# Order and bank use of the first down stage of a pooled-attention and gated-MLP kernel

## The chip, the cores and the metric

The kernel runs on one core of a Trainium2 chip. The metric is the device time in microseconds (us) of one execution; lower is better. The engines have their own instruction queues: TensorE (PE, with its weight loads listed apart as PEld), VectorE (DVE), ScalarE (ACT), GpSimd (POOL) and SyncE (SP, which only issues transfers here). Matmul results go to PSUM, which this kernel splits into three pairs of banks (`banks[0]` to `banks[2]`) and two single banks (`obanks`).

## The reference

Keys and values are averaged over 8 neighbouring positions, attention runs over the 72 pooled positions, and its output goes through two matrix products with g = h cos(h) between them.

```python
# batch 8, heads 8, sequence 576, head_dim 64; d_model 512, d_ff 2048
k_p = k.reshape(B, H, Sp, pool, D).mean(axis=3)      # pool 8, Sp 72
v_p = v.reshape(B, H, Sp, pool, D).mean(axis=3)
scores = scale * np.matmul(q, k_p.transpose(0, 1, 3, 2))
attn = softmax(scores)
attn_out = np.matmul(attn, v_p)
x = attn_out.transpose(0, 2, 1, 3).reshape(B * S, H * D)   # 4608 x 512
h = x @ w_in
g = h * np.cos(h)
return g @ w_out
```

## The kernel before

The 4608 tokens are worked in nine tiles of 512 (`NT`, `TILE`). Each pass t of the main loop (L563) has an up stage and a down stage. The up stage multiplies the tile's columns of `xT` by `w_in` (L354), eight pairs of 512-wide results, each into a bank pair given by `up_bank`; ScalarE takes the cosine (L364) and VectorE multiplies (L368) into `g_sb`. The down stage multiplies `g_sb` by `w_out`. From t = 1 on it is done by seven half-sized products (L432) that need sums of weight blocks, w1 to w4, made by `put_weights` (L388); at t = 0 it is done directly (`down_mm`, L371), 64 matmuls numbered n: 4 row blocks `ms` times 16 chunks `fc`, the chunks lying in four blocks `w_out_sb[0..3]`. Each row block is summed in one PSUM bank, copied out by VectorE (`down_out`, L376) and stored through SP.

Attention is woven into these stages. Batch 0 is worked before the loop (L534 to L560). At t = 0 the down stage also works batch 1: a list `fill` of pairs (n, what) puts pieces ahead of matmul n. `S_(i, bank)` is the scores of part `us[i]` of batch 1: four matmuls (L234) into a bank pair and an exp on ScalarE (L241). `V_(i, bank)` is its values: four matmuls (L269), two Ln (L275) and one exp (L276) on ScalarE for the inverse of the sums, and then a multiply on VectorE in two halves (L280), which reads the bank pair and writes columns of `xT`. With a third argument, the multiply is put into the list `later` and issued by a later entry of `fill`. REST is the remaining 64 rows of batch 0, and `pool_v_mm` pools the values of batch 1.

The schedule is manual: each engine runs its instructions in the order of the code, and waits come from the data and the buffers. So the place of a `put_weights` or of a multiply in the code is its place in VectorE's queue. A bank pair that `values` has used is free once its multiply has read it.

The up stage of t = 1 starts with `up_mm` into `banks[0]`, then `banks[2]`, `banks[1]` and the two `obanks`. Its columns of `xT` are the 64 rows of REST and most of batch 1, so it needs the four multiplies of `us` as well.

At the end of t = 0 GpSimd issues the loads of batch 2 and then pools its keys and values by additions (`pool_first`, L157; `pool_rest`, L163 to L169). The blocks of w_out are loaded by GpSimd's queue in the order 0, 2, 1, 3 (L517 and L522).

The first keys of batch 0 are pooled on TensorE (`pool_k_mm`, L178) and copied into `kk` by `put_kk` (L151) in four casts, all on one engine.

Of the kernel before, what the change touches and what calls it, by code (L numbers as in the profile page):

```python
# [9 lines left out]
FP32 = mybir.dt.float32  # L10
# [10 lines left out]
def kernel(  # L21
# [9 lines left out]
    nc = tc.nc  # L31
    B, H, S, D = q.shape
    Sp = S // POOL
    d_model = H * D
# [112 lines left out]
    def put_kk(b, ps, pj0, pj1, copy):  # L147
        for a in range(2):
            for r in range(2):
                j = key_slot(b, 2 * pj0 + a, r)  # L150
                copy(out=kk[b % 2][half[r], j:j + pj1 - pj0, 0:Sp], in_=ps[half[a]])  # L151

    def pool_first(b, which):

# [16 lines left out]
    def pool_k_mm(b, bank, pj0, pj1):  # L171

        kb = staged["k", b]
        ps = bank[:, 0:(pj1 - pj0) * Sp].rearrange("p (j n) -> p j n", n=Sp)
        for pj in range(pj0, pj1):
            for t in range(ROW):
                for rows in half:
                    nc.tensor.matmul(ps[rows, pj - pj0, :], lhsT=kb[rows, pj, t, :], rhs=groups[rows, t, :],  # L178
                                     start=(t == 0), stop=(t == ROW - 1))
        return lambda copy: put_kk(b, ps, pj0, pj1, copy)  # L180
# [42 lines left out]
    def scores(b, u, pair):  # L223
        scores_mm(b, u, pair)
        scores_exp(b, u, pair)
# [145 lines left out]
        nc.tensor.matmul(o, lhsT=g_sb[:, fc, ms * 128:(ms + 1) * 128],  # L371
                         rhs=w_out_sb[fc // 4][:, fc % 4, :], start=(fc == 0), stop=(fc == FFCH - 1))

    def down_out(t, ms, ps):
        o = msb.tile([128, 2, d_model], FP32, name="o_two", tag="o_two", bufs=2)[:, 0]
        nc.vector.tensor_copy(out=o, in_=ps)  # L376
        rows_of = out.rearrange("(b p t) m -> b t p m", b=B, t=ROW)
        for i, rows in enumerate(half):
            b_, pos = divmod((t * TILE + ms * 128) // 64 + i, ROW)
            nc.sync.dma_start(out=rows_of[b_, ORDER[pos]], in_=o[rows])  # L380
# [151 lines left out]
    early_inverses += ["p1_sb", "v_sb", "q_sb"] * 3  # L532

    warm_up(10, obanks[0])  # L534
    pool_k_mm(0, obanks[1], 0, 2)(vec)
    warm_up(2, banks[1][:, 0, :])
    puts = q_transpose_mm(0, banks[2][:, 0, :], 0, 5), q_transpose_mm(0, obanks[0], 5, 9)
    puts[0](vec)
# [24 lines left out]
    for t in range(NT):  # L563
        b = t + 1
        if t > 0:

            for fp in up_order(t)[0:2]:
                up_mm(t, fp, 0, 2)
        for n, fp in enumerate(up_order(t)):
            up_mm(t, fp, 2 if n < 2 else 0)  # L570
            between = ()
            if t == 0:
                if fp == 4:
                    puts = pool_k_mm(1, obanks[0], 0, 2), pool_k_mm(1, obanks[1], 2, 4)
                elif fp in (5, 6):
                    g0 = 9 * (fp - 5)
                    puts = q_transpose_mm(1, obanks[0], g0, g0 + 5), q_transpose_mm(1, obanks[1], g0 + 5, g0 + 9)
                if fp in (4, 5, 6):
                    puts[0](vec)
                    between = ((puts[1], act),)  # L580
            up_g(t, fp, between)

            late = {5: (1,), 6: (3,)} if t == 1 else {4: (1, 2), 5: (3,)}
            sums = {} if t == 0 else late if b < B else {3: (1, 2), 4: (3,), 5: (4,)}
            put_gs(*[(i, 0) for i in sums.get(n, ())])
            if 0 < t and b < B:
                if n == 0:
                    q_transpose(b)
                    k_transpose(b)
                elif n == 2:  # L590
                    pool_rest(b, "v")
                    if b + 1 < B:
                        nc.gpsimd.tensor_copy(out=gate, in_=kk[b % 2][0:1, H - 1, 0:1])
                        load_q(b + 1)
                        load_kv(b + 1, "v", v)
            if n == 2:
                while stores:
                    stores.pop(0)()
        mms = [(ms, fc) for ms in range(4) for fc in range(FFCH)]
        if t == 0:  # L600
            mms = [(ms, fc) for hm in range(2) for cg in (0, 2, 1, 3) for ms in range(2 * hm, 2 * hm + 2)
                   for fc in range(4 * cg, 4 * cg + 4)]


        def S_(n, bank):
            return lambda: scores(b, us[n], banks[bank])

        later = []

        def V_(n, bank, wait=None):  # L610
            return lambda: values(b, us[n], banks[bank], wait)

        fill = []
        if t < B:
            exp_tables()
            fill = [(1, lambda: scores(t, REST, banks[2])), (16, lambda: values(t, REST, banks[1]))]
        if t == 0:
            fill = [(2, lambda: scores(t, REST, banks[1])), (2, S_(0, 0)), (8, lambda: pool_v_mm(1, banks[2])),
                    (8, lambda: values(t, REST, banks[1])),
                    (8, lambda: put_weights(0, nc.vector, (3, 2))), (8, S_(1, 0)), (8, V_(0, 2)),  # L620
                    (18, S_(2, 1)), (18, lambda: put_weights(0, nc.vector, (4,))),
                    (18, lambda: put_weights(1, nc.vector, (1,))), (21, V_(1, 0, later)), (26, S_(3, 2)), (32, lambda: later.pop()()),
                    (32, V_(2, 1)), (40, V_(3, 0))]
        if t == FIRST:
            early_inverses.clear()
        if t < FIRST:
            fi = 0
            for n, (ms, fc) in enumerate(mms):
                while fi < len(fill) and fill[fi][0] <= n:
                    fill[fi][1]()  # L630
                    fi += 1
                down_mm(obanks[ms % 2], ms, fc)
                if fc == FFCH - 1:
                    down_out(t, ms, obanks[ms % 2])
                if n == 4:
                    put_weights(0, nc.vector, (1,))
                elif n == 36:
                    put_weights(1, nc.vector, (3,))
            put_weights(1, nc.vector, (2, 4))
        else:  # L640
            products, reads = down_products(t)

            def product(i, j=0, k=2 * HF):
                for mm in products[i][j:k]:
                    mm()

            later = []

            u0, u1, u2, u3 = [(b, CHUNKS[i], banks[j]) for i, j in enumerate((2, 1, 0, 1))]
            ur = (t, REST, banks[2])  # L650

            def scores_of(*parts):
                for part in parts:
                    scores_mm(*part)
                for part in parts:
                    scores_exp(*part)

            def muls():
                while later:
                    later.pop(0)()  # L660

            steady, rest = b < B, t < B
            if rest:
                exp_tables()

            product(0, 0, 12)
            product(1, 0, 4)
            product(0, 12)
            reads[0]()
            if steady:  # L670
                scores_of(u0, u1, u2)
            elif rest:
                scores_of(ur)
            product(1, 4)
            if t == 1:
                put_g(2, 0)
            put_gs((1, 1), (2, 1))
            if not steady:
                reads[1]()
            put_gs((3, 1), (4, 1))  # L680
            if steady:
                reads[1]()
                put_g(4, 0)
                values_rows(*u0)
            product(2)
            reads[2]()
            if steady:
                values_rows(*u1)
                values_rows(*u2)
            product(3)  # L690
            reads[3]()
            muls()
            product(4)
            reads[4]()
            muls()
            if steady:
                scores_of(ur, u3)

            product(5, 0, 6)
            if rest:  # L700
                values(*ur, later)
            product(5, 6, 12)
            muls()
            if steady:
                values_rows(*u3)
            product(5, 12)
            reads[5]()
            muls()
            product(6)
            reads[6]()  # L710
        if t < B:
            sin_tables()
        if b + 1 < B:
            if t == 0:
                load_kv(b + 1, "k", k)
                load_q(b + 1)
                load_kv(b + 1, "v", v)
            else:

                nc.gpsimd.tensor_copy(out=gate, in_=g4[0:1, 0, 0:1])  # L720
            pool_first(b + 1, "k")
            if t != 1 and b + 2 < B:
                load_kv(b + 2, "k", k)
            pool_rest(b + 1, "k")
            if t == 1:
                load_kv(b + 2, "k", k)
            pool_first(b + 1, "v")
# [28 lines left out]
```

The softmax here doesn't subtract the row's maximum and nothing guards it: scores larger than these inputs give would overflow.

## Time and profile before

| what | value |
|---|---|
| time, median of 3 runs | 285.4 us (284.73 to 286.28) |
| time of the profiled execution | 284.58 us |
| its span, first to last instruction | 282.8 us |
| granted TensorE clock, mean | 0.999 |
| first down matmul of t = 0 | 33.45 us |
| first up matmul of t = 1 | 53.05 us |
| one down matmul, start to start | 0.216 us |

Times in views count from the start of the span. A timeline row gives the start, the time it covers, the engine, the line, the operation, the written and read tiles, shapes, and the number of instructions merged into it; brackets give the idle time before it and what ended that. In the chain of waits each row is what the end of the program depended on at that time.

### The profile page before, as it was taken

How to read it: one execution, taken by the hardware profiler on the slowest of the kernel's cores; microseconds unless marked ns; L12 is line 12 of the kernel's file. 1: busy time of each engine (PE TensorE's matmuls, PEld its weight loads, DVE VectorE, ACT ScalarE, POOL GpSimd, SP SyncE). 2: the span in 40 equal slices, each digit the busy share in tenths (PEclk: the TensorE clock that was granted, in tenths of full speed). 3: DMA queues.
4: the chain of work that ended last, by engine and by line, in shares of the span. 5: the costliest groups of instructions: out<-in, count | busy, mean ns of one | idle time of the engine just before them, and what ended most of it. 6: DMA issues, size and time to landing. Idle time of an engine off the chain costs nothing.

```text
span 282.8 us, 5887 instructions
## 1 busy us (share of the span) xinstructions
PE 275.2 (97%) x2378; PEld 185.4 (66%) x2378; DVE 212.6 (75%) x313; ACT 167.3 (59%) x199; POOL 132.1 (47%) x146
## 2 busy tenths in 40 slices
PE   7899999999999999999999999999999999999994
PEld 3555554456875687568756975688558855875683
DVE  5448769889946995699568966896689669846972
ACT  3787798368357735774567556655666555436600
POOL 8542114995599259934993389539910000000000
PEclk9999999999999999999999999999999999999999
DMA  7999999795739798997688959882660260005015
GB/s 153 201 206 209 212 207 216 132 190 84 118 60 163 125 215 140 136 175 155 101 148 146 189 80 163 156 174 52 125 148 3 58 148 19 2 21 127 2 37 112
DMA packets 56202, 36.13 MB, mean 128 GB/s; under 512 B 35440, under 2 KB 51312, under 8 KB 56176
## 3 DMA queue, kind: packets, MB, share of 16 engines
q0 software_dynamic: 18208, 18.07, 40.8%
q1 hardware_dynamic: 37328, 17.18, 29.7%
q10 hardware_dynamic: 640, 0.52, 0.8%
q8 instruction: 18, 0.29, 0.4%
q14 instruction: 8, 0.07, 0.1%
HBM read 36.70 MB, written 9.44 MB: 163 GB/s over the span
## 4 chain that ended last, share of the span: by engine, by line
PE 92%; ACT 3%; DMA 2%; DVE 1%; issue 1%; POOL 0%; POOLq 0%; DVEq 0%
PE bank L354 39%; PE obank L432 33%; PE obank L354 5%; PE obank L371 4%; PE bank L234 3%; DMA q_b<-in_q_dram 2%; PE bank L296 2%; PE bank L432 2%; ACT ex L241 1%; PE bank L269 1%; PE obank L178 0%; DVE g_sb L368 0%; PE obank L215 0%; PE bank L186 0%; ACT cos L364 0%
## 5 line engine op out<-in xcount | busy, mean ns | idle before, releaser
L354 PE MATMUL bank<-xT,w_in_sb 128*128 128x512 bf16 x512 | 113.8, 379 | 0.1
L364 ACT ACTIVATE cos<-bank,half_pi 128x1024 f32<-128x1024 f32 x64 | 70.4, 1115 | 55.9 <-PE bank L354 55.9
L354 PEld LDWEIGHTS <-w_in_sb 128*128 128x128 bf16 x576 | 64.9, 113 | 57.4 <-issue 0.3
L368 DVE TENSOR_TENSOR g_sb<-bank,cos 128x1024 bf16<-128x1024 f32 x64 | 77.0, 1221 | 30.5 <-ACT cos L364 30.3
L157 POOL TENSOR_TENSOR half_sums<-kv_st 72x512 f32<-72x512 bf16 x48 | 54.4, 1158 | 8.4 <-DMA kv_st<-in_k_dram 8.0
L241 ACT ACTIVATE ex<-bank 72x1024 bf16<-72x1024 f32 (+1 forms) x40 | 35.0, 931 | 30.0 <-PE bank L234 30.0
L432 PEld LDWEIGHTS <-g 128*128 128x128 bf16 x512 | 47.8, 98 | 5.8
L432 PE MATMUL obank<-w,g 128*128 128x256 bf16 x368 | 42.6, 272 | 0.0
L432 PEld LDWEIGHTS <-g_sb 128*128 128x128 bf16 x384 | 37.0, 98 | 6.4
L163 POOL TENSOR_TENSOR half_sums<-half_sums 72x512 f32<-72x512 f32 x24 | 30.0, 1273 | 0.0
L432 PE MATMUL obank<-w_out_sb,g_sb 128*128 128x256 bf16 x240 | 28.9, 273 | 0.0
L398 DVE TENSOR_TENSOR g<-g_sb 128x1024 bf16<-128x1024 bf16 x32 | 21.9, 685 | 0.3
L720 POOL COPY gate<-g 1x1 bf16<-1x1 bf16 x5 | 0.9, 180 | 37.9 <-DVE inv_rows L299 37.9
L280 DVE TENSOR_TENSOR xT<-bank,inv 64x256 bf16<-64x256 f32 x14 | 5.9, 422 | 15.4 <-ACT inv L276 15.4
L301 DVE TENSOR_TENSOR x_rows<-bank,inv_rows 128x512 bf16<-128x512 f32 x24 | 16.6, 692 | 0.8
L432 PE MATMUL obank<-w_out_sb,g 128*128 128x256 bf16 x112 | 15.6, 273 | 0.0
L432 PE MATMUL obank<-w,g_sb 128*128 128x256 bf16 x128 | 15.3, 272 | 0.0
L371 PE MATMUL obank<-w_out_sb,g_sb 128*128 128x512 bf16 x64 | 15.2, 379 | 0.0
L354 PE MATMUL obank<-xT,w_in_sb 128*128 128x512 bf16 x64 | 15.1, 379 | 0.0
L234 PE MATMUL bank<-qT,kk 64*72 64x128 bf16 (+2 forms) x288 | 12.3, 221 | 0.1
L332 ACT ACT_TABLE_LOAD x9 | 11.5, 1283 | 0.9 <-PEq L740 0.7
L234 PEld LDWEIGHTS <-kk 64*72 64x72 bf16 x288 | 8.7, 110 | 5.1 <-issue 3.4
(99 smaller groups left out, 270.0 us busy)
## 6 DMA issues: line engine op xcount, KB each, us to landing
out_dram<-o_two SPq DMA_DIRECT2D x64, 128.0 KB, 2.4
kv_st<-in_v_dram POOLq DMA_DIRECT2D x8, 576.0 KB, 12.3
kv_st<-in_k_dram POOLq DMA_DIRECT2D x7, 576.0 KB, 8.1
q_b<-in_q_dram POOLq DMA_DIRECT2D x6, 576.0 KB, 7.6
w_in_sb<-in_moe_w_in_dram POOLq DMA_DIRECT2D x4, 512.0 KB, 13.5
w_out_sb<-in_moe_w_out_dram POOLq DMA_DIRECT2D x4, 512.0 KB, 18.6
q_b<-in_q_dram POOLq DMA_DIRECT2D x4, 288.0 KB, 12.3
g_sb<-in_k_dram SPq DMA_DIRECT2D x1, 576.0 KB, 3.4
```

Of the source, the lines that this page charges most:

```text
L157: nc.gpsimd.tensor_tensor(out=s[:, h:h + 2], in0=x[:, h:h + 2, 0:4, :], in1=x[:, h:h + 2, 4:8, :], op=ADD)
L163: add(out=s[:, h:h + 4, 0:2, :], in0=s[:, h:h + 4, 0:2, :], in1=s[:, h:h + 4, 2:4, :], op=ADD)
L234: nc.tensor.matmul(pair[:Sp, bank, c:c + n].rearrange("p (g n) -> p g n", n=64), lhsT=kk[b % 2][half[r], key_slot(b, h0 + i, r), 0:Sp], rh ...
L241: nc.scalar.activation(out=ex[:, 0:nh * n].rearrange("p (a n) -> p a n", a=2), in_=pair[:Sp, :, 0:nh * n // 2], func=ACTF.Exp, scale=scale ...
L301: nc.vector.tensor_tensor(out=x[0:n].rearrange("p (j a d) -> p j a d", j=KCH, a=2), in0=ps[0:n, :, 0:2 * (D + 2)].rearrange("p j (a w) -> ...
L332: nc.scalar.preload_act_table_set("natural_log_exp_and_others")
L354: nc.tensor.matmul(h[j] if h is obanks else h[:, j, :], lhsT=w_in_sb[fc // 4][:, ki, fc % 4:512:4], rhs=xT[:, ki, t * TILE:(t + 1) * TILE] ...
L364: nc.scalar.activation(out=c, in_=ps, func=ACTF.Sin, bias=half_pi[:, :1])
L368: nc.vector.tensor_mul(out=o, in0=ps, in1=c)
L371: nc.tensor.matmul(o, lhsT=g_sb[:, fc, ms * 128:(ms + 1) * 128], rhs=w_out_sb[fc // 4][:, fc % 4, :], start=(fc == 0), stop=(fc == FFCH - 1))
L398: nc.vector.tensor_tensor(out=out[:, f0:f1], in0=x, in1=y, op=op)
L432: mms.append(lambda bank=bank, first=first, g=g, w=w, fc=fc, p=p: nc.tensor.matmul(bank[p], lhsT=g(fc, p), rhs=w(fc), start=(first and fc ...
```

## The change

Four things change, all in the work up to the end of t = 0.

1. `put_kk` takes a pair of copy functions as well; the first keys of batch 0 are copied by VectorE (two casts) and ScalarE (two casts) instead of four on VectorE.
2. The 64 matmuls of the first down stage are ordered so that blocks 0 and 2 of w_out are used for all four row blocks (n = 0 to 31), and then blocks 1 and 3 (n = 32 to 63). So four sums are open at once: in the two `obanks` and in the two halves of `banks[1]`. `down_out` gets its output tile from outside; row blocks 2 and 3 are copied out together after n = 55, block 0 after n = 59, block 1 after n = 63.
3. The attention of batch 1 uses only `banks[0]` and `banks[2]`: scores before n = 2, 8, 28 and 35, values before n = 9, 20, 36 and 44. The postponed multiply is now that of `us[3]`, issued before n = 57; that of `us[1]` is issued at once.
4. The sums of `put_weights(1, ...)`: number 1 goes before n = 20; 3, 2 and 4 together go before n = 38. They stood before n = 18, after n = 36, and after the last matmul.

```diff
-                copy(out=kk[b % 2][half[r], j:j + pj1 - pj0, 0:Sp], in_=ps[half[a]])
+                (copy if callable(copy) else copy[a])(out=kk[b % 2][half[r], j:j + pj1 - pj0, 0:Sp], in_=ps[half[a]])
...
-    def down_out(t, ms, ps):
-        o = msb.tile([128, 2, d_model], FP32, name="o_two", tag="o_two", bufs=2)[:, 0]
+    def down_out(t, ms, ps, o):
         nc.vector.tensor_copy(out=o, in_=ps)
...
-    pool_k_mm(0, obanks[1], 0, 2)(vec)
+    pool_k_mm(0, obanks[1], 0, 2)((vec, act))
...
-        mms = [(ms, fc) for ms in range(4) for fc in range(FFCH)]
-        if t == 0:
-            mms = [(ms, fc) for hm in range(2) for cg in (0, 2, 1, 3) for ms in range(2 * hm, 2 * hm + 2)
-                   for fc in range(4 * cg, 4 * cg + 4)]
...
-        if t == 0:
-            fill = [(2, lambda: scores(t, REST, banks[1])), (2, S_(0, 0)), (8, lambda: pool_v_mm(1, banks[2])),
-                    (8, lambda: values(t, REST, banks[1])),
-                    (8, lambda: put_weights(0, nc.vector, (3, 2))), (8, S_(1, 0)), (8, V_(0, 2)),
-                    (18, S_(2, 1)), (18, lambda: put_weights(0, nc.vector, (4,))),
-                    (18, lambda: put_weights(1, nc.vector, (1,))), (21, V_(1, 0, later)), (26, S_(3, 2)), (32, lambda: later.pop()()),
-                    (32, V_(2, 1)), (40, V_(3, 0))]
...
         if t < FIRST:
-            fi = 0
+            mms = [(ms, 4 * cg + f) for cgs, mss in (((0, 2), (0, 1)), ((0, 2), (2, 3)), ((1, 3), (2, 3, 0, 1)))
+                   for cg in cgs for ms in mss for f in range(4)]
+            acc = [*obanks, banks[1][:, 0, :], banks[1][:, 1, :]]
+            os = [msb.tile([128, 2, d_model], FP32, name="o_two", tag="o_two", bufs=2) for _ in range(2)]
+            fill = [(2, lambda: scores(t, REST, banks[1])), (2, S_(0, 0)),
+                    (4, lambda: put_weights(0, nc.vector, (1,))),
+                    (8, lambda: pool_v_mm(1, banks[2])), (8, lambda: values(t, REST, banks[1])),
+                    (8, lambda: put_weights(0, nc.vector, (3, 2))), (8, S_(1, 0)), (9, V_(0, 2)),
+                    (18, lambda: put_weights(0, nc.vector, (4,))), (20, lambda: put_weights(1, nc.vector, (1,))),
+                    (20, V_(1, 0)), (28, S_(2, 2)), (35, S_(3, 0)), (36, V_(2, 2)),
+                    (38, lambda: put_weights(1, nc.vector, (3, 2, 4))), (44, V_(3, 0, later)), (57, lambda: later.pop()())]
             for n, (ms, fc) in enumerate(mms):
-                while fi < len(fill) and fill[fi][0] <= n:
-                    fill[fi][1]()
-                    fi += 1
-                down_mm(obanks[ms % 2], ms, fc)
-                if fc == FFCH - 1:
-                    down_out(t, ms, obanks[ms % 2])
-                if n == 4:
-                    put_weights(0, nc.vector, (1,))
-                elif n == 36:
-                    put_weights(1, nc.vector, (3,))
-            put_weights(1, nc.vector, (2, 4))
+                while fill and fill[0][0] <= n:
+                    fill.pop(0)[1]()
+                down_mm(acc[ms], ms, fc)
+                if fc == FFCH - 1 and ms != 2:
+                    for m in (2, 3) if ms == 3 else (ms,):
+                        down_out(t, m, acc[m], os[m // 2][:, m % 2])
```

More of the change, by code (lines that the diff above doesn't have):

```diff
@@ L611, in V_ @@
             return lambda: values(b, us[n], banks[bank], wait)
-        fill = []
         if t < B:
             exp_tables()
-            fill = [(1, lambda: scores(t, REST, banks[2])), (16, lambda: values(t, REST, banks[1]))]
-        if t == 0:
-            fill = [(2, lambda: scores(t, REST, banks[1])), (2, S_(0, 0)), (8, lambda: pool_v_mm(1, banks[2])),
-                    (8, lambda: values(t, REST, banks[1])),
-                    (8, lambda: put_weights(0, nc.vector, (3, 2))), (8, S_(1, 0)), (8, V_(0, 2)),
-                    (18, S_(2, 1)), (18, lambda: put_weights(0, nc.vector, (4,))),
-                    (18, lambda: put_weights(1, nc.vector, (1,))), (21, V_(1, 0, later)), (26, S_(3, 2)), (32, lambda: later.pop()()),
-                    (32, V_(2, 1)), (40, V_(3, 0))]
         if t == FIRST:
```

## The prediction

> **What bounds the kernel now.** I read the page's busy times and chain shares first, to see which engine sets the end.
>
> ```profile
> PE 275.2 (97%) x2378; PEld 185.4 (66%) x2378; DVE 212.6 (75%) x313; ACT 167.3 (59%) x199; POOL 132.1 (47%) x146
> PE 92%; ACT 3%; DMA 2%; DVE 1%; issue 1%; POOL 0%; POOLq 0%; DVEq 0%
> ```
>
> TensorE is busy for 97% of the span and is 92% of the chain that ends last. So a microsecond of TensorE idling added anywhere is added to the end, and one removed comes off. The change lies in the first down stage (t = 0). There I read the chain of waits in order of time (start, us, what), from the last attention step of the stage to the next up stage:
>
> ```profile
> 47.38 0.04 issue
> 47.42 0.61 PE bank L269 x4
> 48.03 5.18 PE obank L371 x24
> 53.22 5.18 PE bank L354 x24
> ```
>
> TensorE goes from the last 24 down matmuls (5.18/24 = 0.216 us each) to the up matmuls of t = 1 with no gap. In the timeline that border is at 53.05. Little can be won: from 33.45 to 53.05 I find three idle places, 0.3 us before the pooling of v (it waits for the last g), 0.1 us at the first values of batch 1 (copy of pooled v), and 0.2 us at 47.2. No wait for w_out is among them: the DMA landings put block 2 at 37.50, block 1 at 39.94, block 3 at 42.36, and their first matmuls start at 38.54, 40.27 and 42.88.
>
> The TensorE timeline (start, us, line) gives the slots of the pieces to be moved, from start to start:
>
> ```profile
> 43.41 0.41 PE L234 MATMUL bank<-qT,kk 64*72 64x256 bf16 x4
> 43.75 1.47 PE L371 MATMUL obank<-w_out_sb,g_sb 128*128 128x512 bf16 x6
> 45.05 0.60 PE L269 MATMUL bank<-ex,vz 72*128 72x256 bf16 x4
> 45.49 1.89 PE L371 MATMUL obank<-w_out_sb,g_sb 128*128 128x512 bf16 x8
> ```
>
> A scores piece takes 0.34 (and 0.1 ahead of it), a values piece 0.44. The ScalarE timeline prices what follows them: exp of scores 1.00, two Ln 1.20, the exp of the inverse 0.63.
>
> ```profile
> 44.32 1.00 ACT L241 ACTIVATE ex<-bank 72x1024 bf16<-72x1024 f32 x1
> 45.69 1.20 ACT L275 ACTIVATE v_sb<-bank 64x512 f32<-64x512 f32 x2 [0.37 <-PE bank L269]
> 46.92 0.63 ACT L276 ACTIVATE v_sb<-v_sb 128x512 f32<-128x512 f32 x1
> ```
>
> Last the two queues that turn out to decide, VectorE and GpSimd around the border:
>
> ```profile
> 49.00 1.30 DVE L388 TENSOR_TENSOR w<-w_out_sb,w_out_sb 128x1024 bf16<-128x1024 bf16 x1
> 50.33 1.39 DVE L280 TENSOR_TENSOR xT<-bank,q_sb 64x512 bf16<-64x512 f32 x2
> 52.39 0.69 DVE L376 COPY o_two<-obank 128x512 f32<-128x512 f32 x1 [0.67 <-PE obank L371]
> 53.26 0.69 DVE L376 COPY o_two<-obank 128x512 f32<-128x512 f32 x1 [0.17 <-PE obank L371]
> 53.86 1.67 DVE L388 TENSOR_TENSOR w<-w,w_out_sb 128x1024 bf16<-128x1024 bf16 x1
> 55.56 1.64 DVE L388 TENSOR_TENSOR w<-w_out_sb,w 128x1024 bf16<-128x1024 bf16 x1
> ```
>
> ```profile
> 46.37 4.94 POOL L157 TENSOR_TENSOR half_sums<-kv_st 72x512 f32<-72x512 bf16 x4 [7.99 <-DMA kv_st<-in_k_dram]
> 51.61 0.85 POOL L115 DMA_DIRECT2D kv_st<-in_k_dram  x1 [0.30 <-POOL half_sums L157]
> 52.47 2.50 POOL L163 TENSOR_TENSOR half_sums<-half_sums 72x512 f32<-72x512 f32 x2
> 55.05 2.34 POOL L166 TENSOR_TENSOR ring<-half_sums 72x512 bf16<-72x512 f32 x2
> ```
>
> The reader is to see three things. The last multiply of batch 1 (L280, reading banks[0]) is over at 51.7, before the border, so banks[0], which the first up matmul of t = 1 overwrites, is free. Two weight sums (L388) stand after the border, where nobody waits. And a weight sum that takes 0.69 at 39.8 takes 1.30 to 1.67 beside GpSimd work: L388 waits for a GpSimd instruction to end, then runs its 0.69.
>
> [...] the multiply of L280, with one input in PSUM, stays at 1.39 a pair. [...] the timelines keep program order. [...] In the trace the first warm-up matmuls run at 0.43 each, twice the later 0.216[...].
>
> **The change part by part.** *First keys by two engines.* Now four casts on VectorE, 6.71 to 7.99; then two there and two on ScalarE (1.14/4 = 0.29 each at 27.34), over at about 7.35. But the chain runs through the landing of q at 7.65, the transposes, the copy of qT at 8.19 and the scores at 8.74; VectorE idles 0.2 us before that copy, and ScalarE idles 3.04 us before its own at 8.41. Gain 0; at most 0.2 if q landed earlier, and ScalarE's two casts end long before 8.41, so no loss.
>
> *Order of w_out and four accumulators.* 64 matmuls before and after, no instruction more. The waits for w_out that it could spare are 0 in this execution. The halves of banks[1] are first written at n = 16 (40.2), after the REST multiply has read them at 39.73: no wait. One output tile pair instead of single tiles and the stores issued later: SP's queue idles here, and the second write of those tiles is 15 us later. 0.
>
> *Attention on two bank pairs, step by step.* Up to the second scores nothing moves (they start at 37.63, once the exp has read banks[0]). Matmul n = 8 now goes ahead of the values of us[0], which fills the 0.1 us of idling: n = 8 at 37.97, V0 at 38.19, n = 9 at 38.63, V1 before n = 20 at 41.01, S2 before n = 28 at 43.27 (banks[2] is free at 43.05), n = 34 at 44.92. S3 would start at 45.23 but writes banks[0] and needs the multiply of V1. That one is no longer postponed, yet stands on VectorE behind V0's multiply and two weight sums, which in the trace are over at 44.37; with 1.39 it ends at 45.80. S3 starts at 45.84: 0.6 us of new idling. V2 follows at 46.40, V3 at 48.58, n = 44 at 49.02, and 20 x 0.216 later TensorE reaches the border at 53.35, 0.3 later than now.
>
> *The queue behind it.* ScalarE: exp of S3 46.29 to 47.29, V2's Ln to 48.50, its inverse to 49.16. VectorE waits for that from 45.80 (3.4 us idle), multiplies V2 from 49.20 to 50.59, and then by its order has three weight sums (block pairs 1: 3, 2, 4), the copies of ms 2 and 3, the multiply of V3, and the copies of ms 0 and 1. GpSimd's four L157, spared the wait for the sum at 49.0 (0.48), end at 50.85, the DMA issue runs to 52.0, L163 begins at 52.02. First sum: 0.2 of wait and 0.69, to 51.53. Second: to 52.2. L163 has then been blocked since 52.02 and goes first, as L166 did between the sums at 53.86 and 55.56: 1.2 of wait and 0.69, to 54.1. Copies 2 x 0.71: 55.55. V3's multiply, 1.39: 56.94. Only then may the first up matmul write banks[0] and its later ones read xT: TensorE starts t = 1 at about 56.98 instead of 53.05, having idled some 3.6 us behind the border. The copies of ms 0 and 1 end at 58.4; obanks are wanted 5.2 us after the restart (62.2), banks[1] has been read by 55.55: nothing else is late. Behind the waiting matmul stand all of t = 1's matmuls, and behind them ScalarE's cosines.
>
> Sum: 56.98 - 53.05 = 3.93, of which 0.3 is at the S3 stop (0.6 less the idling saved) and 3.6 at the border. Later stages show no TensorE idling that could absorb it. Bounds of the unknown, the wait for GpSimd: if no sum meets it, VectorE is 1.4 earlier and the sum is 2.5; if each of three sums waits the 0.98 seen at 53.86, it is 5.4. I take 3.9.
>
> The profiled execution (284.58, span 282.8 and 1.8 around it) would become 288.5; the runs shown have a median of 285.4, 0.8 above it, and give 289.3.
>
> **Rivals.**
> A, sums that miss GpSimd (a slightly later L163, or VectorE winning the tie at 52.2): +2.5, 287.9. For it: the two come within 0.2 us. Against it: the blocked GpSimd instruction went first at 55.5.
> B, the idle border (3.4 us without a matmul[...]) also drops the clock[...], +5.6, 291.0. [...]
> C, not slower: w_out's landing. In before, blocks 1 and 3 have slack of 0.33 and 0.52 us; after, they are wanted at n = 32 and 48, over 4 us after landing. If in ordinary executions they land later than in the profiled one, before stalls and after doesn't. It decides only from a lateness of 4.2 us (3.9 + 0.33) on, where it gives 285.4. Against it: the runs spread over only 1.5 us, and block 2, with 0.47 us of slack after, would stall both.
> D, the change doesn't do what it says: if the multiply of V3 came to VectorE ahead of the sums, the border would move by 0.3 to 0.8 only (285.9). The order in the code is plain: fill 38 before fill 57.
>
> **How the numbers follow.** Forecast 289.3: 0.58. A 0.19, B 0.15, C 0.04, D 0.04. Range 287.5 to 291.3: A and B with 0.3 to 0.4 of scatter. A measurement of this kernel tells about 0.5% (1.4 us) from no change: C splits into 0.02 faster and 0.02 same, D is same, the rest slower: 0.02, 0.06, 0.92.
>
> **What would show it.** On TensorE, one idle stretch of about 3.4 us before the first L354 of t = 1, released by L280, and one of 0.6 before S3 near 45.2. On VectorE, idling from 45.8 to 49.2, then L388 three times, L376 twice, L280 twice, L376 twice to about 58.4. First scores still at 8.74. The prediction is wrong if L280 of V3 ends before 54, if TensorE's idling has another releaser, or if the up matmuls behind it show 0.43 (B).

## The result, and the profile after

The changed kernel takes 293.49 us (median of 6 runs, 293.22 to 293.79) beside 285.06 before in the same comparison: a ratio of 1.0296, 95% interval 1.0267 to 1.0325. It is slower, as forecast, by 8.4 us instead of 3.9, and outside the range.

On the page of the changed kernel, these are the busy times, the shares of the chain by engine, and the clock line (tenths of full clock in 40 slices):

```profile
PE 275.0 (94%) x2356; PEld 185.6 (64%) x2378; DVE 213.0 (73%) x311; ACT 168.0 (58%) x201; POOL 131.6 (45%) x146
PEclk9999999869999999999999999999999999999999
PE 85%; DVE 5%; ACT 5%; DMA 2%; issue 2%; POOL 0%; POOLq 0%
```

TensorE's work is the same, its share of the chain has fallen from 92% to 85%, and VectorE has come in with 5%. The clock line has a dip in the eighth and ninth slice, between 51 and 66 us. The chain of waits in order of time (start, us, what) shows both places. Rows of "issue", 0.01 to 0.05 us each, are left out here; the border is the start of t = 1 on TensorE.

```profile
49.37 0.68 DVE xT L280
50.06 0.69 DVE xT L280
50.79 0.70 DVE w L387
51.52 3.46 DVE w L387
55.00 1.63 DVE w L387
56.67 1.29 DVE o_two L375 x2
57.99 0.68 DVE xT L280
58.68 0.70 DVE xT L280
59.43 6.99 PE bank L354 x24
```

Before, this stretch was TensorE all through. Now it is VectorE's queue in exactly the predicted order: the multiply of us[2], three weight sums (L387, formerly L388), the two copies, the multiply of us[3]; and only then the up matmuls. The second sum takes 3.46 instead of 0.69. GpSimd's timeline shows what stood beside it, a DMA issue and then two additions (L163); the sum ends, at 54.97, some 0.6 after them:

```profile
51.05 0.85 POOL L115 DMA_DIRECT2D kv_st<-in_k_dram  x1 [0.30 <-POOL half_sums L157]
51.92 2.49 POOL L163 TENSOR_TENSOR half_sums<-half_sums 72x512 f32<-72x512 f32 x2
```

And the first 24 up matmuls take 6.99 us where they took 5.18. The waits of TensorE (total us, how many, longest us) and the stages by time (length, then busy time of PE, PEld, DVE, ACT and POOL, granted clock, DMA share, GB/s) say why:

```profile
PE bank L354 <- DVE xT L280: 5.8, 1, 5.8
PE bank L234 <- DVE xT L280: 0.5, 1, 0.5
```

```profile
59.40:62.80 3.40, 3.37 (x8) 1.17 (x9) 1.29 (x2) 0.00 (x0) 3.40 (x4) 0.50 0.94 199
62.80:66.40 3.60, 3.60 (x18) 1.93 (x17) 1.38 (x2) 2.12 (x2) 2.30 (x2) 1.00 1.01 196
```

TensorE waited 5.8 us at the border (and 0.5 at S3, the scores of us[3]), and ran the first 3.4 us behind it at half clock. The trace's clock record has half clock from 55.94 to 62.77: the granted clock is 0.50 in that stretch, and 1.00 in the 3 us on either side of it.

The account of the two profiled executions, span 291.4 against 282.8: the first down matmul comes 0.15 later (q landed later); S3's stop and the new slots cost 0.28; the border wait 5.95 (the last down slot ends at 53.48, the first up matmul starts at 59.43); the half clock 1.64 (the down stage of t = 1 starts 15.46 behind the first up matmul, 13.82 before); between the last read of a sum and the end lie 4.3 us instead of 3.7, a difference of the last store. These add up to 8.6. Between the half clock and the last read nothing is gained or lost.

### The profile page after: what moved, and what is told of

It reads as the page before. It is cut to its first block, busy times and chain, and to the rows that moved or that the text cites. A ratio compares the mean times of both kernels' runs of the same rounds, so it can differ in the third digit from the quotient of the medians.

```text
span 291.4 us, 5864 instructions
## 1 busy us (share of the span) xinstructions
PE 275.0 (94%) x2356; PEld 185.6 (64%) x2378; DVE 213.0 (73%) x311; ACT 168.0 (58%) x201; POOL 131.6 (45%) x146
## 4 chain that ended last, share of the span: by engine, by line
PE 85%; DVE 5%; ACT 5%; DMA 2%; issue 2%; POOL 0%; POOLq 0%
PE bank L354 38%; PE obank L431 32%; PE obank L354 5%; PE bank L234 3%; DVE w L387 2%; DMA q_b<-in_q_dram 2%; PE bank L296 2%; ACT ex L241 2%; PE bank L431 2%; DVE xT L280 2%; PE bank L269 1%; ACT v_sb L275 1%; DVE o_two L375 0%; PE obank L178 0%; DVE g_sb L368 0%
## 5 line engine op out<-in xcount | busy, mean ns | idle before, releaser
L163 POOL TENSOR_TENSOR half_sums<-half_sums 72x512 f32<-72x512 f32 x24 | 30.0, 1272 | 0.0
```

The costliest lines, as they stand in the source:

```text
L163: add(out=s[:, h:h + 4, 0:2, :], in0=s[:, h:h + 4, 0:2, :], in1=s[:, h:h + 4, 2:4, :], op=ADD)
```

## The experiments

All start from the changed kernel unless said otherwise. Ratios are to the kernel before, on the same chip.

**1. Is the half clock a cost of its own?** Filler matmuls keep TensorE busy during the wait.

```diff
+        if t == 1:
+            warm_up(24, banks[2][:, 0, :])
         if t > 0:
             for fp in up_order(t)[0:2]:
                 up_mm(t, fp, 0, 2)
```

> The changed kernel with 24 filler matmuls (0.216 us each, 5.2 us in all, into banks[2], which the second up pair overwrites) issued ahead of the first up matmul of t = 1, so that TensorE is busy while it waits for the multiply of us[3]. My theory: the half clock after the border is the price of 6 us of idling. Then the border stays at about 59.4, the clock stays at 1.00, the down stage of t = 1 starts 1.6 us earlier (73.3 instead of 74.9) and the time falls from 293.5 to 291.9. Rival (the half clock costs nothing, since the up stage waits for cosines anyway): 293.5, down stage at 74.9.

291.66 us, ratio 1.023 (1.0195 to 1.0265). TensorE's timeline in the run with the filler:

```profile
53.27 5.34 PE L527 MATMUL bank<-g 128*128 128x512 bf16 x24
59.68 5.37 PE L354 MATMUL bank<-xT,w_in_sb 128*128 128x512 bf16 x24 [1.06 <-DVE xT L280]
```

The border is as late as without the filler (0.25 later), but the 24 up matmuls take 5.37, the down stage of t = 1 starts 13.84 us behind the border instead of 15.46, the mean granted clock is 0.998 instead of 0.988, and 1.8 us are gone from the time. So the half clock is a cost of its own, and here it came with the idling: TensorE idles 1.06 us in this run, 5.80 without the filler. That is as my theory had it.

**2. The three weight sums behind the last copy.**

```diff
-                    (38, lambda: put_weights(1, nc.vector, (3, 2, 4))), (44, V_(3, 0, later)), (57, lambda: later.pop()())]
+                    (44, V_(3, 0, later)), (57, lambda: later.pop()())]
...
+            put_weights(1, nc.vector, (3, 2, 4))
```

> The changed kernel with only the three weight sums 3, 2, 4 of pair 1 moved behind the last copy of the stage. My theory (the sums ahead of the multiply of us[3] are the loss): the copies of ms 2 and 3 run 52.0 to 53.3, the multiply of us[3] 53.4 to 54.7, the border is at about 54.8, clock 1.00; the sums then run beside GpSimd until about 61 and hold up the first products of g, worth 0 to 2 us. Time 286.8 to 289. Rival (four open accumulators and two bank pairs are the loss, whatever the sums do): 292 or more, border at 58 or later.

286.59 us, ratio 1.0053 (1.0037 to 1.0070), a little below the range that I expected. The border is at 54.65, TensorE waits 1.1 us there, and the clock is full (the 24 up matmuls take 5.37 us, the mean clock is 0.999). Seven of the 8.4 us are gone with the place of three instructions; most of the rest is that 1.1 us, and in the order of VectorE's queue it comes from the two copies that still stand ahead of the multiply. That the sums run behind the border until 59.7 costs nothing that the trace shows.

**3. The sums alone, put into the kernel before.** Its banks, accumulators and attention stay as they were.

```diff
-                elif n == 36:
-                    put_weights(1, nc.vector, (3,))
-            put_weights(1, nc.vector, (2, 4))
+                elif n == 37:
+                    put_weights(1, nc.vector, (3, 2, 4))
```

> The kernel before, its banks, accumulators and attention as they were, with only the three weight sums 3, 2, 4 of pair 1 put together behind the multiply of us[2], ahead of that of us[3]. My theory (the place of the sums is the loss, not the banks): the first takes 1.3 us, one of the others meets GpSimd's DMA issue and takes about 3.5, the multiply of us[3] ends near 57, the up stage of t = 1 starts some 4 us later than 53.05 behind an idle TensorE, and the clock halves: 289.5 to 291. Rival (the new banks are the loss): 286 or less.

290.74 us, ratio 1.0202 (1.0170 to 1.0235). VectorE's timeline:

```profile
50.32 1.52 DVE L388 TENSOR_TENSOR w<-w,w_out_sb 128x1024 bf16<-128x1024 bf16 x1
51.88 3.62 DVE L388 TENSOR_TENSOR w<-w_out_sb,w 128x1024 bf16<-128x1024 bf16 x1
55.52 1.39 DVE L280 TENSOR_TENSOR xT<-bank,q_sb 64x512 bf16<-64x512 f32 x2
```

Without any of the new banks the same kind of loss appears, some 6 us of the 8.4: a sum of 3.6 us, the multiply of us[3] over at 56.9, TensorE waiting for it 3.4 us, and a lowered clock (the 24 up matmuls take 8.02 us instead of 5.34, the mean clock is 0.985). Experiments 2 and 3 together show that the place of the sums is the cause of most of the loss, and the four accumulators are not.

**4. Are the sums slow because of GpSimd?** Its pooling is held back until the last sum is written.

```diff
+            if t == 0:
+                nc.gpsimd.tensor_copy(out=gate, in_=w4[1][0:1, 0, 0:1])
             pool_first(b + 1, "k")
```

> The changed kernel, GpSimd's pooling of batch 2 held back until the fourth weight sum of pair 1 is written (a copy of one element of it ahead of the pooling), so that no weight sum meets a GpSimd instruction. My theory: the three sums take 0.69 each, 50.8 to 52.9, the multiply of us[3] ends at 55.6, the border is at 55.7, and with 2.1 us of idling the clock stays full: 287.7, unless the pooled keys of batch 2, some 6 us later, are awaited at t = 1 (seen as a wait of TensorE near 72). Rival (the sums are slow for another reason, such as the landing of the loads): sum 2 still takes over 2 us and the border is at 59.

VectorE's timeline in that run:

```profile
50.38 0.69 DVE L387 TENSOR_TENSOR w<-w_out_sb,w_out_sb 128x1024 bf16<-128x1024 bf16 x1
51.11 0.69 DVE L387 TENSOR_TENSOR w<-w,w_out_sb 128x1024 bf16<-128x1024 bf16 x1
51.84 0.69 DVE L387 TENSOR_TENSOR w<-w_out_sb,w 128x1024 bf16<-128x1024 bf16 x1
```

Three times 0.69, where the changed kernel has 0.69, 3.45 and 1.63, and the border at 55.33: the meeting with GpSimd is the whole excess. The time was another than expected: 289.99 in the median, ratio 1.0150 (1.0090 to 1.0209). Three of the four executions, with a mean clock of 0.993 to 0.994, took 289.87 to 290.46; the fourth, at 0.999, took 287.81, which is the expected time. In the trace, of one of the three, TensorE waits 2.09 us at the border and the 24 up matmuls behind it take 7.06 us, where they took 5.37 in experiments 1 and 2. So the clock dropped after idling of 2.1 us there and, by time and mean clock, in two more executions, but not in the fourth. My expectation that it would stay full, which no trace had shown, was wrong.

**5. Why did one sum take 3.45?** First, the DMA issue between the two kinds of GpSimd additions is moved behind them.

```diff
-            if t != 1 and b + 2 < B:
+            if t > 1 and b + 2 < B:
                 load_kv(b + 2, "k", k)
             pool_rest(b + 1, "k")
-            if t == 1:
+            if t <= 1:
                 load_kv(b + 2, "k", k)
```

> The changed kernel with the issue of the next keys' load moved on GpSimd from between L157 and L163 to behind L166, so that L163 follows L157 directly and meets the first sum. It tells why sum 2 took 3.45 us. Theory X (the DMA issue makes VectorE's request stand behind more than one GpSimd instruction): sum 1 now waits for one L163 only and takes about 1.9, and sum 2 likewise. Theory Y (two L163 in a row are not parted by a waiting sum): sum 1 waits for both and takes 3.1. In both the border stays between 58 and 60 and the time near 293.

292.02 us, ratio 1.0243 (1.0208 to 1.0278). VectorE, then GpSimd:

```profile
50.59 1.84 DVE L387 TENSOR_TENSOR w<-w_out_sb,w_out_sb 128x1024 bf16<-128x1024 bf16 x1
52.47 1.64 DVE L387 TENSOR_TENSOR w<-w,w_out_sb 128x1024 bf16<-128x1024 bf16 x1
54.14 1.63 DVE L387 TENSOR_TENSOR w<-w_out_sb,w 128x1024 bf16<-128x1024 bf16 x1
```

```profile
50.62 2.94 POOL L163 TENSOR_TENSOR half_sums<-half_sums 72x512 f32<-72x512 f32 x2
53.63 2.31 POOL L166 TENSOR_TENSOR ring<-half_sums 72x512 bf16<-72x512 f32 x2
```

The first sum gets in between the two L163 (which stretch from 2.49 to 2.94): theory Y falls, X stands so far. Each sum now waits for about one addition: they take 0.94 to 1.15 more than 0.69, and an L163 takes 1.27 in the changed kernel.

**6. Does the DMA issue itself block the sum?** It stays where it was; the first L163 is held back until the sums are over.

```diff
+            if t == 0:
+                nc.gpsimd.tensor_copy(out=gate, in_=w4[1][0:1, 0, 0:1])
             pool_rest(b + 1, "k")
```

> The changed kernel, with GpSimd held back between its DMA issue and its first L163 until the fourth weight sum of pair 1 is written; the DMA issue itself stays at 51. It tells what sum 2 waited for. Theory X1 (the DMA issue itself keeps VectorE's sum from starting, until 51.9): sum 2 takes 0.9 to 1.1. Theory X2 (the issue blocks nothing; the L163 queued behind it has the turn): sum 2 takes 0.69. In both the sums are over by about 53.3, the multiply of us[3] ends near 56, and the time is 288 to 290.5, by whether the clock halves.

287.89 us, ratio 1.0118 (1.0084 to 1.0152), just under what I expected. GpSimd's issue and VectorE's second sum:

```profile
51.25 0.85 POOL L115 DMA_DIRECT2D kv_st<-in_k_dram  x1 [0.30 <-POOL half_sums L157]
```

```profile
51.53 0.69 DVE L387 TENSOR_TENSOR w<-w,w_out_sb 128x1024 bf16<-128x1024 bf16 x1
```

The sum runs in 0.69 in the midst of the issue: theory X2. The issue by itself held up nothing here; in the changed kernel the sum, with 3.45, waits for the L163s that stand behind it. How it comes to wait stays open in two points. In the changed kernel the sum was due at 51.52 and the first L163 is recorded only from 51.92, so the sum might have gone first. And two L163 pass a waiting sum when the issue stands ahead of them (3.45 to 3.63 in the changed kernel and in experiments 1 and 3), but only one in experiment 5, where it doesn't.

**7. The multiply ahead of the sums**, as `(44, V_(3, 0))`, with the sums right behind it.

> The changed kernel with the multiply of us[3] not postponed, so that it stands on VectorE ahead of the three weight sums, which stay ahead of the four copies. My theory: the multiply ends at about 52.6 and TensorE goes into t = 1 at 53.4 without idling; what is late next is the copies of ms 2 and 3, behind the sums, at 57 to 59, while the third up pair wants banks[1] at 57: a wait of 0 to 2 us there, no half clock: 285.3 to 287.3. Rival (taking the multiply out of the way only moves the whole loss to the copies): 289 or more.

287.88 us, ratio 1.0095 (1.0066 to 1.0125): a little above what I expected. TensorE enters t = 1 at 53.67 without idling, and stops where expected, at banks[1]:

```profile
59.18 1.89 PE L354 MATMUL bank<-xT,w_in_sb 128*128 128x512 bf16 x8 [1.90 <-DVE o_two L375]
```

The copies stand behind sums of 2.54, 1.64 and 0.69. The 2.54 is again a sum that was passed by the second L163: it was due at 52.86, while the first one (from 52.35) ran, and ended at 55.40, after the second, which ended at 54.85.

**8. The first keys alone**, the kernel before with `((vec, act))`.

> The kernel before with only the first keys copied by two engines. My theory (it is off the chain, which runs through the landing of q): the four casts end about 0.6 us earlier, the first scores start at the same distance behind the landing of q, the time is that of before within 0.3 us. Rival (a gain, or a loss from a second engine to wait for): over 0.5 us either way.

285.19 against 284.60 us, ratio 1.0015 (1.0002 to 1.0027). ScalarE's timeline:

```profile
7.55 0.56 ACT L151 CAST kk<-obank 64x144 bf16<-64x144 f32 x2 [2.12 <-DVE kk L151]
```

The two engines don't work side by side: ScalarE's casts wait for VectorE's (6.82 to 7.45), to which the profile puts the wait down, so the four end at 8.11 instead of 7.99, not 0.6 earlier. The first scores stand 1.04 us behind the first transposes in both kernels. The ratio leaves room for a cost of 0.1 to 0.8 us, but no wait in the trace carries one.

**9. A better order for VectorE**: the multiply of us[1] ahead of sums, three sums in VectorE's idling, the multiply of us[3] not postponed, two sums behind the last copy.

```diff
-                    (18, lambda: put_weights(0, nc.vector, (4,))), (20, lambda: put_weights(1, nc.vector, (1,))),
-                    (20, V_(1, 0)), (28, S_(2, 2)), (35, S_(3, 0)), (36, V_(2, 2)),
-                    (38, lambda: put_weights(1, nc.vector, (3, 2, 4))), (44, V_(3, 0, later)), (57, lambda: later.pop()())]
+                    (20, V_(1, 0)), (21, lambda: put_weights(0, nc.vector, (4,))),
+                    (22, lambda: put_weights(1, nc.vector, (1, 3))), (28, S_(2, 2)), (35, S_(3, 0)), (36, V_(2, 2)),
+                    (44, V_(3, 0))]
...
+            put_weights(1, nc.vector, (2, 4))
```

> The changed kernel with VectorE's queue put in another order: the multiply of us[1] ahead of the weight sums, sums 4 of pair 0 and 1 and 3 of pair 1 in VectorE's idling at 45 to 48.5, the multiply of us[3] not postponed, sums 2 and 4 of pair 1 behind the last copy. My theory: S3 no longer waits (0.5 us), the multiply of us[3] ends at about 52, TensorE reaches t = 1 without idling at 52.9, clock 1.00, the time is 284.5 to 285.2, that of before or up to 0.5 better. Rival (four accumulators cost something by themselves): 286 or more.

284.69 against 284.60 us, ratio 1.0001 (0.9984 to 1.0019): with the sums and multiplies in this order, the four accumulators and the two bank pairs cost nothing that can be measured here; the interval leaves room for 0.5 us.

**10. The same order with the first keys copied by VectorE alone.**

> The reordered version (multiply of us[1] ahead, sums in VectorE's idling, the last two sums behind the copies) with the first keys copied by VectorE alone, as before. My theory: the copies by two engines neither help nor hurt, and the reordered version is worth at most 0.5 us: ratio to before 0.998 to 1.001. Rival (the second engine costs the 0.15% that it seemed to cost alone): ratio below 0.998.

284.35 against 284.91 us, ratio 0.9983 (0.9969 to 0.9997), the best of all. The border in its trace:

```profile
50.70 1.89 PE L371 MATMUL obank<-w_out_sb,g_sb 128*128 128x512 bf16 x8
52.43 5.34 PE L354 MATMUL bank<-xT,w_in_sb 128*128 128x512 bf16 x24
```

It is at 52.43, 0.6 before that of the kernel before, and the time gains 0.17%, at the edge of what can be measured. Whether the second engine at the keys costs anything, these two intervals, which overlap, don't settle.

## Why the prediction was wrong in size

**The attention step by step: right.** Every row of VectorE's queue stands in the predicted order, and up to the first sum no time is off by more than 0.2 us: S3 waited 0.5 (predicted 0.6), VectorE idled 3.44 (3.4), the multiply of us[2] ended at 50.76 (50.59), and the down matmuls ended 0.28 later than before, as the predicted 0.3.

**The queue behind it: the term that was mis-sized is the wait for GpSimd.** I put the sums at 0.2 + 0.69, 0.69, and 1.2 + 0.69, 3.5 us in all. They took 0.69, 3.45 and 1.63, 5.85 us from the start of the first to the end of the third. The failing step is "Second: to 52.2": I took the second sum to start freely, since GpSimd was at its DMA issue then. It was due in the midst of that issue, and waited for both L163 behind it. Experiments 3 and 4 show that this meeting is the excess, 6 that the issue alone doesn't make it, and 5 that a wait for additions comes without an issue ahead too. The 2.35 us that the sums took beyond my 3.5, and the 1.64 of half clock, make up most of the difference between 3.9 and 8.4. My upper bound, 5.4 for a wait of one addition at each sum, was the nearest to what the border moved, 6.2 (0.28 and 5.95); but I took 3.9 as likeliest, since the one tie seen in the trace of before had GpSimd pass only once.

**Rival B was the case that held, on top of it.** I gave the half clock a chance of 0.15 and 1.7 us (B's 5.6 less 3.9), an estimate of mine that no trace had shown. The size came out right, 1.64, and 1.8 in experiment 1; the chance was too low. In the trace of before the longest wait of TensorE is 1.5 us, at the start, so it couldn't tell what a wait like the forecast 3.6 does. In the changed kernel half clock was granted at 55.94, 2.3 us after TensorE's last down matmul, and experiment 4 shows a lowered clock with only 2.1 us of idling. I also kept B apart from the upper bound of the wait, while the second brings the first with it: every trace with 3.4 us or more of idling shows the lowered clock (the changed kernel with 5.80, experiments 3 with 3.41 and 5 with 5.13), those with about 2 us only in part (4 with 2.09, but not 6 with 2.17 and 7 with 1.90). With both, 285.4 + 5.4 + 1.7 = 292.5, which would have come within 1 us of the measured time, and my range ended at 291.3.

**The parts costed at nothing:** order of w_out, four accumulators and stores, right (experiment 9). The reason for the stores was wrong: SP's queue does not idle all through the stage. It issued stores from 45.13 to 55.57 before, and from 57.39 to 62.51 in the changed kernel; no wait of TensorE in the trace comes from them. The first keys, right that nothing is gained, wrong on the way: they are not over 0.6 earlier, because the engines took turns. Rivals A and D: experiment 6, with sums that meet next to nothing, gave the 287.9 of A (sums that miss GpSimd), and D (the multiply ahead of the sums) fell with the order that the trace shows. C (w_out landing late) needed landings 4.2 us late; the largest wait for w_out that a trace shows is 0.4 us (experiment 2).

## What to carry to other kernels

On a kernel that one engine bounds, an instruction that nobody waits for is still dear when it stands, in another engine's queue, ahead of one that the bound engine needs (7 of the 8.4 us here, by experiment 2): put such work behind the last needed instruction, or into a gap where that queue waits anyway. Before moving a VectorE operation like these sums, with two SBUF inputs, look up what GpSimd is doing at the new place, and count its queued instructions, not just the one running: a sum of 0.69 us took up to 3.63 beside GpSimd's additions, while the multiplies and copies that read PSUM kept their 1.39 and 1.29 a pair. And where a wait on TensorE like those seen here is forecast, add the half clock that can follow (it cost 1.64 us behind a wait of 5.80, and came in experiment 4 behind one of 2.09) to the same case instead of keeping it as a rival.

## What the runs showed of the hardware that was not expected

- Idling of 2.09 us was followed by a lowered clock, and the length of the idling alone doesn't tell whether the clock drops. For the kernel before and each trace with a wait right at the border, this is how long TensorE waited ahead of the up stage of t = 1, what the 24 up matmuls behind that wait took, and the mean granted clock of the execution:

  | run | wait, us | 24 up matmuls, us | mean clock |
  |---|---|---|---|
  | before | none | 5.34 | 0.999 |
  | experiment 1 | 1.06 | 5.37 | 0.998 |
  | experiment 2 | 1.08 | 5.37 | 0.999 |
  | experiment 4 | 2.09 | 7.06 | 0.993 |
  | experiment 6 | 2.17 | 5.37 | 0.996 |
  | experiment 3 | 3.41 | 8.02 | 0.985 |
  | experiment 5 | 5.13 | 6.70 | 0.994 |
  | changed kernel | 5.80 | 6.99 | 0.988 |

  In experiment 7 the wait of 1.90 us comes after 16 of the 24, and the 8 behind it take 1.89, as the 8 after them do: the clock stayed full. Another execution of experiment 6, which took 289.37 at a mean clock of 0.990, looks as if the clock had dropped, but has no trace. Nor do the 24 take longer the longer the wait: they are slowest behind 3.41 us. In the changed kernel half clock was granted for 6.83 us, 3.34 of them after the matmuls were back. What decides whether the clock drops, and for how long, was not shown. The ends of matmuls are modelled in the traces.
- A VectorE sum that waits for GpSimd is not always next: two GpSimd additions of 1.27 each ran while it waited (3.45 to 3.63 for a sum of 0.69), when a DMA issue stood directly ahead of them; in experiment 5, without it, one ran.
- Casts by VectorE and ScalarE out of the two halves of one PSUM bank ran one after the other (6.82 to 7.45, then 7.55 to 8.11), although they read different partitions. Both write `kk`, and the profile puts ScalarE's wait down to VectorE's cast into it, so this may be the program's order and no limit of the chip; what makes the second wait was not tried.
